# A fused attention and MLP kernel on one core: q/k weights loaded on ScalarE's queue, a run's product behind the gate, more moves on SyncE, and a reordered end

## The chip, the cores and the metric

The kernel runs on one core of a Trainium2 chip. The core has a matrix engine (TensorE, PE in the profile), VectorE (DVE), ScalarE (ACT), GpSimd (POOL) and SyncE (SP), each with its own instruction queue, and 16 DMA engines that move data between the chip's memory and SBUF, the on-chip memory. Matmul results go to PSUM, which has eight banks. A queue works in order: an instruction that waits holds up all behind it on the same engine. SP and ACT can issue DMAs, and so can POOL. The metric is the time of one execution in microseconds (us); "before" has a median of 200.42 us over three runs (200.35 to 201.31).

## The reference: what is computed

With `x` of 2048 positions and 512 columns in bf16, layer-normalised to `xn`:

```python
qkv = xn @ wqkv                                  # 32 heads of 16
logits[w] = q[s] . k[s - 2*w] * 16**-0.5         # w = 0..7, positions below 0 masked
s = (softmax(logits) . v) @ wo                   # sliding, dilated attention

h  = gelu(layernorm(xn) @ w1)                    # four column groups shifted by -1, +1, -2, +2
x1 = xn + shifted(h) @ w2
b  = x1 + gelu(layernorm(x1) @ w3) @ w4          # inner width 1376

out = x + s * silu(b)
```

The sliding window steps by two positions, so even and odd positions are two separate sequences; the kernel calls them p = 0 and p = 1, each with 1024 rows.

## The kernel before

**First part, to about 104 us.** The rows come in as `xn` tiles of 128 rows (`load_x`, L115). A chunk c is 512 rows of one sequence, and chunk 0 is loaded tile by tile, the others two tiles at a time. On SP the order is: two tiles of chunk 0, the first half of the q/k weights `wqk_sb` (L129), a tile, the second half, the last tile, then chunks 1 and 2, `w1` and chunk 3. Each half of the weights has two of the four blocks of 128 contraction rows, 512 KB; a tile of x has 128 KB. DVE and ACT normalise the tiles, TensorE transposes them (`first_columns`, L272, and `columns`, L259), and `qk` (L282) makes q and k. Its very first group of matmuls takes the blocks of the first weight half for two outputs, and then those of the second half. After it come w1, the shifted w2 and w3 for all four chunks, with gelu on ACT.

**The loop, n = 0 to 15.** The attention is done in 17 units (`order`, L56). Unit 0 has the first 64 rows of both sequences, every other unit 120 rows of one. Iteration n issues, in this order on the engines: `scores(n)` on TensorE (L605); `weighted(n-1)` (L638), which multiplies the weights `prob` with the values (L652) and takes the result out of PSUM bank o into `orw`: on DVE a small copy `mix` (L667) and an add (L668), and a wide copy, the "eviction" (`evict`), that is on ACT in the loop (L670); the exponentials on ACT (L616); `values(n+1)` on TensorE into bank b (L584); the gate of an earlier tile on DVE (L563); `within(n)`, the band mask, on DVE (L625); `w4_part(n)` on TensorE (L531) with its add on DVE (L539); and from n = 6 on `final`, the product with `wo` for one tile (L801, also in bank b), whose result DVE multiplies with the gate (L812), and POOL adds x (L817). All instructions of an engine keep the order of the source.

**Runs.** `orw` holds sums and row sums side by side. For a run (two units in a row; units 0 and 13 to 16 are runs of their own), the sums have to get into `oT`, with heads on the partitions: eight DMAs, one for each group of four heads (`moves`, L687; on SP and POOL). The row sums go out to `dn` (`sums_gather`), are inverted on DVE (L760) and written to memory, and are read back broadcast over the partitions (`sums_read`, L768, on SP). Then DVE multiplies `oT` by them: `sums_apply`, L776. With the run's last unit b, this is done in iteration b + 3, behind `within` and ahead of the add of `w4_part`. Head group 7 is moved one iteration after the others, ahead of `sums_read` on SP.

**The end, from n = 15 on.** The last runs have no time for those DMAs. R is 11, so R-3, R-2 and R-1 are the runs of units 14, 15 and 16, and R-4 that of unit 13. For R-3 to R-1 TensorE turns the row sums (`sums_turn`, L706), DVE inverts them (`sums_inverse`, L714), ACT spreads them (L719), TensorE turns them back (`sums_back`, L744) and DVE multiplies (`sums_mult`, L753). For R-2 and R-1, TensorE also does the move (`rows`, L731), with a copy on ACT (L736). `gate2` to `gate7` are the last six tiles; tile 7 is done in two halves of 256 columns, each added on DVE and stored from SP or ACT. For tile 6 the add of x is done by TensorE and ACT (`pe_add`, L831). In this part the eviction of unit 15 is on DVE (L671), and `load_xo` and `store` are DMAs on SP.

Of the kernel before, what the change touches and what calls it, by code (L numbers as in the profile page):

```python
# [15 lines left out]
def kernel(  # L16
# [19 lines left out]
    W = 8  # L36
# [87 lines left out]
    wqk_sb = midt([P, ND, 2 * D], "wqk_sb")  # L124
    x_tiles = load_x(0, 1)
    next(x_tiles)
    next(x_tiles)
    for dt in range(0, ND, 2):
        sp.dma_start(out=wqk_sb[:, dt : dt + 2, :], in_=wqkv_v[:, dt : dt + 2, 0 : 2 * D])  # L129
        next(x_tiles)  # L130
    list(load_x(1, 2))
# [12 lines left out]
    eps = const.tile([P, 1], F32, name="eps")  # L144
    dve.memset(eps[:], EPS)

    wm = psa("warm_ps")
# [489 lines left out]

    def weighted(n, eng=None):  # L638

# [19 lines left out]
        if p is None:  # L659
# [4 lines left out]
            t.tensor, t.offset + off, [list(t.ap[0]), [step, 2], list(t.ap[-2]), [1, width]]  # L664
        )
        mix = small.tile([P, 2 * ND, W], F32, name="mix", tag="mix")
        dve.tensor_copy(out=mix, in_=ov_[:, 1, :, 0:W])  # L667
        dve.tensor_tensor(out=ow[:, :, c + m : c + KB], in0=ov_[:, 0, :, m:KB], in1=mix, op=ALU.add)  # L668
        if eng is None:
            return lambda: act.activation(wide(ow, c, KB, m), wide(ov_, 0, CH + W, m), AF.Copy)  # L670
        return lambda: eng.tensor_copy(out=wide(ow, c, KB, m), in_=wide(ov_, 0, CH + W, m))  # L671

# [97 lines left out]

    def sums_apply(i):
        _, a, b, _, rw, parts = run_of(runs[i][0])
        rr = rden.pop(i).rearrange("p (s q) -> p s q", s=ND)
        for p, q0, c, nq in parts:
            o = oT[p][:, :, q0 : q0 + nq]
            dve.tensor_tensor(out=o, in0=o, in1=rr[:, :, c : c + nq], op=ALU.mult)  # L776

# [13 lines left out]
    def final(p, i, tags="b"):  # L791
# [15 lines left out]
        def mult(k, cs, pt):  # L807
# [8 lines left out]
            def add(eng):  # L816
                eng.tensor_tensor(out=x_o[:, cs], in0=sg, in1=x_o[:, cs], op=ALU.add)  # L817
                if len(pts) > 1:
                    (sp, act)[k % 2].dma_start(out=ov[p, i * P : (i + 1) * P, cs], in_=x_o[:, cs])

            return add

        def gate(eng):
            for k, (cs, pt) in enumerate(pts):
                gate.add = mult(k, cs, pt)
                if eng is not None:
                    gate.add(eng)

        return gate

    def pe_add(p, i, sg, tag):  # L831

        x_o = xo[p, i & ~1][:, i % 2, :]
        pt = pst(tag, "add_ps")[:, 0, :]
        pe.matmul(pt, lhsT=ident[:], rhs=x_o, start=True, stop=False)

        def rest():
# [5 lines left out]
    def store(q, p, i, n=2):  # L843
        q.dma_start(
                out=ov[p, i * P : (i + n) * P, :].rearrange("(i q) d -> q i d", q=P),
                in_=xo[p, i & ~1][:, i % 2 : i % 2 + n, :],
            )

# [6 lines left out]
    for n in range(NN - 1):  # L855
# [20 lines left out]
        for i in back:  # L876
            if 0 < i < R - NC - 1:
                moves(i, [sp], None, [7])
            sums_read(i)
        for i in done:  # L880
            if i == 0:
                moves(i, [sp, pool], 0)
            elif i < R - NC - 1:
                moves(i, [pool, sp, pool, pool, sp, pool, sp], None, range(7))
            elif i == R - NC - 1:
                moves(i, [pool], None, range(4))
            else:
                moves(i, [pool, pool, sp, pool])
        if n == NN - 2:
# [3 lines left out]
        late = [i for i, (a, b) in enumerate(runs) if n == max(b + 3, 5)]  # L893
        if n < NN - 2:
            for i in late:
                sums_apply(i)
        w4_part(n, 0, NF if n < NN - 2 else CUT)
# [8 lines left out]
        if gate:  # L906
            gate(pool)
        if n == NN - 3:
            moves(R - NC - 1, [pool], None, range(4, 8))
# [5 lines left out]
    scores(NN - 1)  # L915
    weighted(NN - 2, dve)()
    load_xo(1, 6)
    store(sp, 1, 0)
    exps(NN - 1)
    act.preload_act_table_set("silu_and_others")  # L920
    w4_part(NN - 2, CUT, NF)
    gate_silu(NN - 2)
    within(NN - 1)
    gate2 = final(1, 2, "b")
    layout("high", f=1, g=1, h=1, i=1)
    sums_turn(R - 2, "g")
    sums_inverse(R - 2, rows(R - 2, "h"))
    gate2(pool)
    sums_back(R - 3, "f")
    evict = weighted(NN - 1)  # L930
    sums_apply(R - 4)
    sums_mult(R - 3)
    evict()
    gate_silu(NN - 3)
    gate3 = final(1, 3, "i")
    gate3(pool)
    store(sp, 1, 2)
    gate4 = final(1, 4, "w")
# [57 lines left out]
```

## Time and profile before

| | us |
|---|---|
| median of three runs | 200.42 (200.35 to 201.31) |
| the profiled execution | 201.85 |
| its span, first to last instruction | 200.1 |
| TensorE busy | 188.8 (94%) |
| DVE busy | 127.0 (63%) |
| ACT busy | 125.3 (63%) |
| POOL busy | 63.5 (32%) |

The granted TensorE clock was 0.996 of full. All times in the text are from the start of the span. A line such as "140.75 0.66 DVE L776 TENSOR_TENSOR oT<-oT,orw ... [1.50 <-DMA orw<-rden_d]" says: at 140.75 us, for 0.66 us, on DVE, from line 776, tile `oT` made of `oT` and `orw`; ahead of it the engine was idle for 1.50 us, and that ended with the landing of a DMA into `orw`. SPq and ACTq are an engine's queue issuing a DMA, which is not counted as busy. In a list of waits the three numbers are the total, the number of waits and the longest. The chain of waits is followed back from the last instruction, at each step to what released it.

### The profile page before, as it was taken

To read this page: it belongs to the slowest core of one execution; us is meant where nothing else is said; L and a number is where in the kernel's file an instruction comes from. 1 tells how busy PE (TensorE), PEld (TensorE's weight loads), DVE (VectorE), ACT (ScalarE), POOL (GpSimd) and SP (SyncE) were. 2 spreads that over 40 slices of the span, in tenths; PEclk is the share of its full clock that TensorE was granted. 3 is DMA by queue.
4 is the path that set the end of the run, shared out by engine and by line. 5 is a ranking of instruction groups with operands and counts; after the bars stand their busy time and mean duration, and the time that the engine had idled before them with its cause. 6 is when DMAs were issued, how large, how long until landed. Compare 5 with 4: busy or idle time off the path is not lost.

```text
span 200.1 us, 6140 instructions
## 1 busy us (share of the span) xinstructions
PE 188.8 (94%) x2563; PEld 98.5 (49%) x2589; DVE 127.0 (63%) x250; ACT 125.3 (63%) x137; POOL 63.5 (32%) x121
## 2 busy tenths in 40 slices
PE   7699999999999999999999999999899999999790
PEld 2488754444444444444445555455455555555450
DVE  4688876228449968200005777786878787878982
ACT  3279849645820534666568788877757776677921
POOL 4055724700200120100000704124426262669460
PEclk9999999999999999999999999999999999999998
DMA  5973181479262266340510113122232251523443
GB/s 165 336 233 98 45 275 55 132 186 349 64 156 56 105 144 169 109 105 0 178 58 0 21 15 79 59 54 59 52 111 50 56 156 49 157 44 97 121 157 108
DMA packets 32748, 22.32 MB, mean 112 GB/s; under 512 B 17072, under 2 KB 31696, under 8 KB 32720
## 3 DMA queue, kind: packets, MB, share of 16 engines
q1 hardware_dynamic: 30960, 20.71, 35.9%
q0 software_dynamic: 1472, 1.02, 2.6%
q8 instruction: 20, 0.33, 0.7%
q10 hardware_dynamic: 288, 0.20, 0.3%
q14 instruction: 8, 0.07, 0.1%
HBM read 12.41 MB, written 4.83 MB: 86 GB/s over the span
## 4 chain that ended last, share of the span: by engine, by line
PE 76%; DMA 8%; DVE 5%; ACT 4%; SPq 3%; issue 2%; DVEq 0%; ACTq 0%
PE w_ps L396 17%; PE qk_ps L299 14%; PE w_ps L531 12%; PE w_ps L356 7%; PE w_ps L332 7%; PE v_ps L584 7%; DMA oT<-orw 4%; PE wo_ps L801 4%; PE o_ps L652 3%; DMA wqk_sb<-in_A_wqkv_dram 3%; ACT orw L670 2%; PE s_ps L605 2%; SPq L682 1%; PE w_ps L412 1%; PE tr_ps L266 1%
## 5 line engine op out<-in xcount | busy, mean ns | idle before, releaser
L616 ACT ACTIVATE prob<-s_ps 128x2048 bf16<-128x2048 f32 (+1 forms) x18 | 32.0, 1781 | 18.8 <-PE s_ps L605 18.8
L531 PE MATMUL w_ps<-w_sb,h3T 128*128 128x512 bf16 (+1 forms) x174 | 40.4, 379 | 0.3 <-issue 0.3
L696 POOL DMA_DIRECT2D oT<-orw x46 | 23.6, 519 | 49.8 <-DVE orw L660 30.3
L400 ACT ACTIVATE h3T<-w_ps 128x1024 bf16<-128x1024 f32 x20 | 20.5, 1024 | 24.9 <-PE w_ps L396 24.9
L396 PE MATMUL w_ps<-x1nT,w_sb 128*128 128x512 bf16 x156 | 34.8, 379 | 0.2
L299 PE MATMUL qk_ps<-xnT,wqk_sb 128*128 128x256 bf16 (+1 forms) x191 | 29.3, 308 | 1.3 <-DMA wqk_sb<-in_A_wqkv_dram 0.8
L531 PEld LDWEIGHTS <-h3T 128*128 128x128 bf16 (+1 forms) x176 | 17.0, 98 | 20.4
L396 PEld LDWEIGHTS <-w_sb 128*128 128x128 bf16 x160 | 15.5, 98 | 19.1 <-issue 0.4
L299 PEld LDWEIGHTS <-wqk_sb 128*128 128x128 bf16 x192 | 18.4, 98 | 11.1 <-DMA wqk_sb<-in_A_wqkv_dram 1.1
L625 DVE TENSOR_TENSOR prob<-prob,band 128x2048 bf16<-128x2048 bf16 (+1 forms) x18 | 21.4, 1191 | 2.3 <-ACT prob L616 2.3
L306 ACT ACTIVATE qT<-qk_ps,sel 128x1024 bf16<-128x1024 f32 x16 | 16.7, 1113 | 6.3 <-PE qk_ps L299 6.3
L584 PE MATMUL v_ps<-wv_sb,xnT 128*128 128x512 bf16 x49 | 15.8, 381 | 1.4 <-DVE sg L812 0.6
L801 PE MATMUL wo_ps<-wo_sb,oT 128*128 128x512 bf16 (+1 forms) x67 | 16.2, 366 | 0.9 <-DVE oT L776 0.7
L361 DVE TENSOR_TENSOR xn<-w_ps,xn 128x1024 bf16<-128x1024 f32 x8 | 9.7, 1211 | 11.5 <-PE w_ps L356 11.5
L817 POOL TENSOR_TENSOR xo<-sg,xo 128x512 bf16<-128x512 bf16 x9 | 10.4, 1153 | 20.7 <-DVE sg L812 20.2
L587 DVE CAST v_aug<-v_ps 128x512 bf16<-128x512 f32 x1 | 0.7, 692 | 22.5 <-ACT h3T L400 22.5
L356 PE MATMUL w_ps<-w_sb,hT 128*128 128x512 bf16 x63 | 14.3, 379 | 0.1
L332 PE MATMUL w_ps<-xn2T,w_sb 128*128 128x512 bf16 x62 | 14.2, 379 | 0.1
L539 DVE TENSOR_TENSOR xn<-w_ps,xn 128x512 bf16<-128x512 f32 x15 | 10.3, 690 | 5.9 <-PE w_ps L531 5.8
L670 ACT ACTIVATE orw<-o_ps 128x896 bf16<-128x896 f32 x15 | 13.7, 913 | 0.3 <-issue 0.3
L652 PE MATMUL o_ps<-prob,v_aug 64*32 64x64 bf16 x1088 | 12.5, 196 | 0.4 <-DVE prob L625 0.3
L215 POOL TENSOR_SCALAR l3r<-l3m 128x4 f32<-128x4 f32 x4 | 0.9, 229 | 35.9 <-DVE l3m L211 35.9
(99 smaller groups left out, 242.9 us busy)
## 6 DMA issues: line engine op xcount, KB each, us to landing
x1n_dram<-xn SPq DMA_DIRECT2D x4, 512.0 KB
xo<-in_A_x_dram SPq DMA_DIRECT2D x8, 256.0 KB
out_dram<-xo SPq DMA_DIRECT2D x7, 256.0 KB
xn<-in_A_x_dram SPq DMA_DIRECT2D x6, 256.0 KB
orw<-rden_d SPq DMA_DIRECT2D x6, 240.0 KB
w_sb<-in_B_w_dram SPq DMA_DIRECT2D x1, 1376.0 KB
w_sb<-in_B_w_dram SPq DMA_DIRECT2D x1, 1280.0 KB
wqk_sb<-in_A_wqkv_dram SPq DMA_DIRECT2D x2, 512.0 KB
```

The costliest lines, as they stand in the source:

```text
L299: pe.matmul(pt[:, b, :], lhsT=wqk_sb[:, dt, nt * P : (nt + 1) * P], rhs=xnT[p][:, dt, ms], start=(dt == 0), stop=(dt == ND - 1),)
L332: pe.matmul(pt[:, b, :], lhsT=w1_sb[:, dt, g * P : (g + 1) * P], rhs=xn2T[:, dt, :], start=(dt == 0), stop=(dt == ND - 1),)
L356: pe.matmul(pt[:, j, :], lhsT=w2_src(p, g, m0), rhs=w2_sb[:, g, :], start=(g == 0), stop=(g == ND - 1),)
L396: pe.matmul(pt[:, b, :], lhsT=w3_sb[:, dt, ft * P : (ft + 1) * P], rhs=x1nT[:, dt, :], start=(dt == 0), stop=(dt == ND - 1),)
L400: act.activation(h3_tile(c)[:, 2 * a : 2 * a + 2, :], pt, AF.Gelu_apprx_tanh)
L531: pe.matmul(pt, lhsT=h3[c][:fs, ft, jj * P : (jj + 1) * P], rhs=w4_sb[:fs, ft, :], start=(ft == 0), stop=(ft == NF - 1 and t < NN - 2),)
L584: pe.matmul(vp, lhsT=xnT[p][:, dt, k0 : k0 + P], rhs=wv_sb[:, dt, :], start=first, stop=last)
L616: act.activation(pr[:, rs_], t[:, rs_], AF.Exp, scale=SCALE)
L625: dve.tensor_tensor(out=w, in0=w, in1=b.unsqueeze(1).to_broadcast([P, m, KB]), op=ALU.min)
L652: pe.matmul(op[32 * cg : 32 * cg + 32, s, g * KB : (g + 1) * KB], lhsT=va[KB * s : KB * s + KB, dt * 8 + h, :], rhs=pr[KB * s : KB * s + K ...
L696: queues[hh % len(queues)].dma_start(out=oT[p][DH * hh : DH * (hh + 1), :, q0 : q0 + nq], in_=w[32 * cg : 32 * cg + DH, ND * jj : ND * jj ...
L801: pe.matmul(pt, lhsT=oT[p][:, dt, i * P : (i + 1) * P], rhs=wo_sb[:, dt, cs], start=(dt == 0), stop=(dt == ND - 1),)
```

## The change

Six things, in the order of the source.

1. All x tiles are issued on SP without the weights between them. The two DMAs of the q/k weights are issued on ACT, after the load of its table, and a memset of one column of each block by DVE comes ahead of them, which they have to wait for.
2. In the loop, up to n = 13, `sums_apply` of a run comes behind `final` and its gate.
3. Of a run's eight moves POOL issues 0, 2 and 4 and SP 1, 3 and 5, and then 6 and 7 one iteration later (before: POOL four, SP three, then one). For unit 14 in iteration 15, POOL and SP issue four each (before: six and two).
4. The eviction of unit 15 is on ACT behind the exponentials, not on DVE.
5. The end has a new order. Two things of it are new work for an engine: `sums_apply(R - 4)` is on POOL, and the first half of tile 7 is added by TensorE and ACT, as tile 6 is.
6. Both row copies come behind the spread sums on ACT (before: that of R-2 came ahead).

```diff
     wqk_sb = midt([P, ND, 2 * D], "wqk_sb")
-    x_tiles = load_x(0, 1)
-    next(x_tiles)
-    next(x_tiles)
-    for dt in range(0, ND, 2):
-        sp.dma_start(out=wqk_sb[:, dt : dt + 2, :], in_=wqkv_v[:, dt : dt + 2, 0 : 2 * D])
-        next(x_tiles)
+    list(load_x(0, 1))
     list(load_x(1, 2))
...
+    dve.memset(wqk_sb[:, :, 0:1], 0.0)
+    for dt in range(0, ND, 2):
+        act.dma_start(out=wqk_sb[:, dt : dt + 2, :], in_=wqkv_v[:, dt : dt + 2, 0 : 2 * D])
...
-    def weighted(n, eng=None):
+    def weighted(n, first=lambda: None):
...
+        first()
         mix = small.tile([P, 2 * ND, W], F32, name="mix", tag="mix")
...
-    def sums_apply(i):
+    def sums_apply(i, eng=dve):
...
-    def pe_add(p, i, sg, tag):
+    def pe_add(p, i, tag, cs):
...
-                moves(i, [sp], None, [7])
+                moves(i, [sp], None, [6, 7])
...
-                moves(i, [pool, sp, pool, pool, sp, pool, sp], None, range(7))
+                moves(i, [pool, sp], None, range(6))
...
             else:
-                moves(i, [pool, pool, sp, pool])
+                moves(i, [pool, sp])
...
         within(n, 2 if n == 0 else 1)
         late = [i for i, (a, b) in enumerate(runs) if n == max(b + 3, 5)]
-        if n < NN - 2:
-            for i in late:
-                sums_apply(i)
         w4_part(n, 0, NF if n < NN - 2 else CUT)
...
         if gate:
             gate(pool)
+        if n < NN - 2:
+            for i in late:
+                sums_apply(i)
...
     scores(NN - 1)
-    weighted(NN - 2, dve)()
+    evict = weighted(NN - 2)
     load_xo(1, 6)
     store(sp, 1, 0)
     exps(NN - 1)
+    evict()
     act.preload_act_table_set("silu_and_others")
...
     gate2 = final(1, 2, "b")
     layout("high", f=1, g=1, h=1, i=1)
+    sums_back(R - 3, "f")
+    gate3 = final(1, 3, "h")
+    sums_apply(R - 4, pool)
+    evict = weighted(NN - 1, first=lambda: gate2(pool))
+    evict()
     sums_turn(R - 2, "g")
-    sums_inverse(R - 2, rows(R - 2, "h"))
-    gate2(pool)
-    sums_back(R - 3, "f")
-    evict = weighted(NN - 1)
-    sums_apply(R - 4)
-    sums_mult(R - 3)
-    evict()
-    gate_silu(NN - 3)
-    gate3 = final(1, 3, "i")
+    sums_inverse(R - 2, rows(R - 2, "i"), True)
     gate3(pool)
     store(sp, 1, 2)
     gate4 = final(1, 4, "w")
+    sums_mult(R - 3)
+    sums_turn(R - 1, "g")
     sums_back(R - 2, "f")
+    sums_inverse(R - 1, rows(R - 1, "h"), True)
     sums_mult(R - 2)
-    sums_turn(R - 1, "g")
+    gate_silu(NN - 3)
     gate5 = final(1, 5, "b")
-    sums_inverse(R - 1, rows(R - 1, "i"), True)
     gate4(pool)
     gate5(pool)
     store(sp, 1, 4)
-    sums_back(R - 1, "h")
-    gate6 = final(1, 6, "w")
+    sums_back(R - 1, "i")
+    gate6 = final(1, 6, "g")
     sums_mult(R - 1)
+    halves = [slice(0, D // 2), slice(D // 2, D)]
+    add6 = pe_add(1, 6, "o", slice(0, D))
     gate6(None)
-    add6 = pe_add(1, 6, gate6.sg, "g")
-    gate7 = final(1, 7, "fb")
-    add6()
+    gate7 = final(1, 7, "fw")
+    add6(gate6.sg)
     store(act, 1, 6, 1)
-    gate7(dve)
+    add7 = pe_add(1, 7, "h", halves[0])
+    gate7.mult(0)
+    add7(gate7.sg)
+    store(sp, 1, 7, 1, halves[0])
+    gate7.mult(1)(dve)
+    store(act, 1, 7, 1, halves[1])
```

More of the change, by code (lines that the diff above doesn't have):

```diff
@@ L668, in weighted @@
         dve.tensor_tensor(out=ow[:, :, c + m : c + KB], in0=ov_[:, 0, :, m:KB], in1=mix, op=ALU.add)
-        if eng is None:
-            return lambda: act.activation(wide(ow, c, KB, m), wide(ov_, 0, CH + W, m), AF.Copy)
-        return lambda: eng.tensor_copy(out=wide(ow, c, KB, m), in_=wide(ov_, 0, CH + W, m))
+        return lambda: act.activation(wide(ow, c, KB, m), wide(ov_, 0, CH + W, m), AF.Copy)
     oT = {}
@@ L775, in sums_apply @@
             o = oT[p][:, :, q0 : q0 + nq]
-            dve.tensor_tensor(out=o, in0=o, in1=rr[:, :, c : c + nq], op=ALU.mult)
+            eng.tensor_tensor(out=o, in0=o, in1=rr[:, :, c : c + nq], op=ALU.mult)
     def slot():
@@ L817, in add @@
                 eng.tensor_tensor(out=x_o[:, cs], in0=sg, in1=x_o[:, cs], op=ALU.add)
-                if len(pts) > 1:
-                    (sp, act)[k % 2].dma_start(out=ov[p, i * P : (i + 1) * P, cs], in_=x_o[:, cs])
             return add
@@ L827, in gate, with rest @@
                     gate.add(eng)
+        gate.mult = lambda k: mult(k, *pts[k])
         return gate
-    def pe_add(p, i, sg, tag):
-        x_o = xo[p, i & ~1][:, i % 2, :]
-        pt = pst(tag, "add_ps")[:, 0, :]
+    def pe_add(p, i, tag, cs):
+        x_o = xo[p, i & ~1][:, i % 2, cs]
+        pt = pst(tag, "add_ps")[:, 0, cs]
         pe.matmul(pt, lhsT=ident[:], rhs=x_o, start=True, stop=False)
-        def rest():
+        def rest(sg):
             pe.matmul(pt, lhsT=ident[:], rhs=sg, start=False, stop=True)
@@ L841, in pe_add, with store @@
         return rest
-    def store(q, p, i, n=2):
+    def store(q, p, i, n=2, cs=slice(0, D)):
         q.dma_start(
-                out=ov[p, i * P : (i + n) * P, :].rearrange("(i q) d -> q i d", q=P),
-                in_=xo[p, i & ~1][:, i % 2 : i % 2 + n, :],
-            )
+            out=ov[p, i * P : (i + n) * P, cs].rearrange("(i q) d -> q i d", q=P),
+            in_=xo[p, i & ~1][:, i % 2 : i % 2 + n, cs],
+        )
     final_at = {n: divmod(n - 6, 8) for n in range(6, 16)}
```

## The prediction

> **What bounds the kernel now.** I read the page first, for the busy shares and the granted clock, then the chain of waits in order of time, TensorE's own waits, and the timeline of the three places where TensorE stands still.
>
> ```profile
> span 200.1 us, 6140 instructions
> ...
> PE 188.8 (94%) x2563; PEld 98.5 (49%) x2589; DVE 127.0 (63%) x250; ACT 125.3 (63%) x137; POOL 63.5 (32%) x121
> ```
>
> TensorE is busy for 188.8 of 200.1 us at a granted clock of 0.996. No matmul of the main body goes away, so all that can be won is in the 11.3 us in which it stands, or is handed out again there. The chain says where the kernel follows something other than TensorE:
>
> ```profile
> 2.70 5.42 DMA wqk_sb<-in_A_wqkv_dram
> ...
> 8.17 2.36 PE qk_ps L299 x20
> ...
> 184.78 1.00 DVE orw L671
> 185.77 1.73 DVE prob L625
> ...
> 194.30 1.09 DVE slots L810 x2
> ```
>
> The q/k weights hold the start, and VectorE (DVE) holds the end from 182.7 on. TensorE's waits put prices on the places:
>
> ```profile
> PE qk_ps L299 <- DMA wqk_sb<-in_A_wqkv_dram: 0.8, 1, 0.8
> PE wo_ps L801 <- DVE oT L776: 0.7, 1, 0.7
> PE v_ps L584 <- DVE sg L812: 0.6, 1, 0.6
> ```
>
> The third one is in the loop. In the timeline a run's product L776 stands on DVE until its row sums arrive, so L539 and the gate L812 are late, and the next `values` matmul finds bank b still in use:
>
> ```profile
> 140.75 0.66 DVE L776 TENSOR_TENSOR oT<-oT,orw 128x960 bf16<-128x960 bf16 x1 [1.50 <-DMA orw<-rden_d]
> ...
> 142.66 1.02 PE L584 MATMUL v_ps<-wv_sb,xnT 128*128 128x512 bf16 x3 [0.59 <-DVE sg L812]
> ```
>
> The end, from the timeline:
>
> ```profile
> 184.69 1.08 DVE L671 CAST orw<-o_ps 128x896 bf16<-128x896 f32 x1
> ...
> 185.24 1.17 POOL L817 TENSOR_TENSOR xo<-slots,xo 128x512 bf16<-128x512 bf16 x1
> ...
> 185.69 1.81 DVE L625 TENSOR_TENSOR prob<-prob,band 128x2048 bf16<-128x2048 bf16 x1
> ...
> 189.18 0.37 SPq L789 DMA_DIRECT2D xo<-in_A_x_dram  x1
> ...
> 196.80 0.34 ACTq L819 DMA_DIRECT2D out_dram<-xo  x1
> ```
>
> L625 takes 1.81 us here and 1.21 in every other iteration: it meets POOL's L817 for 0.7 us and loses 0.6. L563 (0.63 alone, 0.93 at 158.94 beside L817) and the half-size L776 at 188.98 (0.89, where 960 elements take 0.66) show the same. A DVE operation with two SBUF inputs stands while POOL runs a tensor operation; L812, which reads PSUM, keeps 0.68. POOL can lose too: L216 takes 1.87 at 22.40 beside DVE's L315, else 0.72.
>
> **The change, part by part.**
>
> *Start.* Two 0.43 us issues leave SP, so the x tiles behind them are issued up to 0.9 us earlier. That is worth nothing by itself: from 8.17 to 14 TensorE stands for less than 0.1 us, and SP is idle from 8.5 to 13.07. On ScalarE (ACT) the two issues lie ahead of the first root at 4.12, on DVE the memset (0.06, as L143) ahead of an idle stretch. What counts is when the second weight half lands, since TensorE waits from 7.35 to 8.17. Its issue was at 2.70. It now follows the memset (about 1.1) and may have to stand behind the table load that ends at 2.07, so the halves go out at 1.2 and 1.65 or at 2.1 and 2.55. Against this, the x tiles no longer queue behind the weights but move beside them. Before, 1408 KB had moved when that half was in (three tiles of 128, two halves of 512). Shared byte for byte from the second tile on it is 128 + 2048 = 2176 KB. Shared row for row it is 1664, for a row of weights has 1024 columns and a row of x 512. At the 365 GB/s of 4 to 8 us these are 2.2 and 0.7 us later, less the 0.5 to 1.0 by which the issues are earlier. The other end is the whole wait, 0.8 us gained, if whole transfers alternate. No row of this trace has two queues loading at once. Rows being what the engines move one by one, I take the middle: 0.7 less 0.7, **0.0**; ends -0.8 and +2.2.
>
> The Trainium skill (DMA: Bandwidth & Descriptors, "Queues, rings and completion order") says that each DMA engine goes round the queues packet by packet, a packet being some 9 to 17 descriptors. One tile (128 rows over 16 engines) or one half (256) is about that, so by this rule the old order would stay, and this term would be -0.8.
>
> *Loop.* The product of a run goes behind the gate. The 1.50 us stand then lies where bank b is already free: **-0.6**. What comes late instead is the next iteration's `mix` L667. Its DVE work has 0.57 idle before L539 and 0.24 before L812 (156.46 and 157.40), and `values` starts 0.10 after L812, so 0.9 us of delay costs nothing. The product now stands beside POOL's L817. If DVE is first (it needs no semaphore, and POOL started 0.08 after L812's end at 163.45), `mix` is 0.15 late: cost 0. If POOL is first, the product waits 1.15 and `mix` is 1.35 late: 0.45 each in four iterations (7, 9, 11, 13), +1.8. I take **0.0**, as DVE is the nearer one.
>
> The Trainium skill (SBUF — State Buffer, "SBUF: two separate sides") calls the pair of ports that DVE and GpSimd share an exclusive lock, held for an instruction by whichever starts first. The rows above agree; by it this term is 0 as well, and +1.8 if POOL's start comes first.
>
> Of a run's eight moves, SP issues five (four before) and POOL three. One more SP issue (0.65) lies ahead of the row-sum read L768, which waits for its own write anyway (4.9 us in all); if it is late by all of 0.65, the product that reads it is 1.8 us later than before (163.3 for 161.5 in iteration 11). Cost 0.
>
> *End*, in times of this trace. (1) POOL issues 8 moves instead of 10 (L696, 0.51 each) and is free at 184.2, so its L817 runs from 184.4 to 185.6 and no longer meets L625. That starts at 185.65, when L616's `prob` is done (183.75 + 1.86), and ends at 186.86 instead of 187.50: -0.64. Run 7's product, now on POOL (1.08, from 1.15 for 512 columns), must not come first. Its row sums are requested at 182.63; 240 KB of them took 4.3 and 5.3 us (157.21 to 161.51, 135.46 to 140.75), a single move 2.1, so 120 KB arrive between 184.7 and 187.9, with 186.3 in the middle. If they are early, L625 ends at 187.9. (2) The copy L671 (1.08) goes from DVE to ACT as L670 (0.91). L625 waits for `prob` whichever it is, so nothing is won there. ACT's table load and Silu come 0.9 later, and the next eviction starts at 188.4 instead of 188.88. (3) DVE's list behind `mix` and the add, which end at 188.3 (188.81 before): two reciprocals 0.7, three gates 1.95, three products L753 1.95, L810 0.68 + 0.42 + 0.42, one half add 0.29, together 6.4. Of the 7.96 before, L776 (0.89), one half add and the 0.40 stand ahead of it are gone, and one reciprocal has moved in. With 0.3 of waits for ACT's copies the list ends at 195.0, not 196.77. (4) ACT now has the last word: copy of tile 6 (0.60) to 195.05, its store's issue 0.38, a half copy 0.35, and the last store is issued at 195.85, where the last one was at 196.80: -0.95. (5) Two more moves on SP (0.65 each) push the last x load from 189.18 to 190.5. It arrives 2.4 (the first tile, 0.80 to 3.17) to 2.8 us later, near 193.2; TensorE's add would want it at 192.75: +0.25. End: **-0.7**, from -0.95 to +0.4.
>
> Four more half matmuls (0.22 each) lie in TensorE's idle end.
>
> Sum: 0.0 - 0.6 - 0.7 = -1.3. The profiled execution took 201.85 (span 200.1 and 1.75 around it), 0.7% over the median of 200.42. It becomes 200.55, and the median **199.1**.
>
> **The rivals.**
>
> *Weights sooner.* Whole transfers alternate and the 0.8 wait goes: 198.3. For it: the issues are up to a microsecond earlier, and the engines moved only 184 GB/s from 3 to 4 us. Against: the weights now share from their first row.
>
> *Weights late (slower).* Byte-for-byte sharing brings the second half 2.2 later: 199.1 + 2.2 = 201.3, and 202 if the table load holds the issue as well. It decides once that half lands more than 1.3 us later, after 9.5. For it: the engines are full from 4 us on, so what x gains the weights lose. Against: weight rows are twice as long.
>
> *POOL first in the loop.* +1.8 gives 200.9. For it: POOL held the port in every meeting of the loop. Against: there DVE arrived in the middle of L817.
>
> *No gain at the end.* The row sums of run 7 arrive before 185.6, POOL takes the port ahead of L625, and the end is at +0.3 instead of -0.7: 200.1. For it: the lower bound of 184.7. Against: the 4.3 us and more of the larger reads.
>
> **How the numbers follow.** 0.5% of 200.42 is 1.0 us, about what a measurement of this kernel can tell from no change. Forecast 0.40 (198.6 to 199.6, three quarters of it below 199.4), weights sooner 0.20, no gain at the end 0.15, POOL first 0.13, weights late 0.12. Faster: 0.30 + 0.20 = 0.50. Slower: 0.07 of the weights and 0.03 of POOL, 0.10. The rest, 0.40, is within 0.5%. From weights sooner to POOL first the range is 198.2 to 200.9; left out are the late weights and what lies beyond the ends.
>
> **What would show it.** Start: the wait of L299 for `wqk_sb`, 0.82 now; gone means weights sooner, over 2 means late. Loop: no L584 wait for L812, L776 with no stand ahead of L812; L776 at over 1.5 us would be POOL first. End: L625 at 185 or so back at 1.21, L776 on POOL behind it, last store issued 0.7 to 0.95 earlier, counted from L625's start. The prediction is wrong if TensorE waits more than 2 us for the weights, or if the end moves to ACT's row copies or to the last x load and gives back more than 0.7.

## The result, and the profile after

The changed kernel takes 203.45 us in the median (201.80 to 205.02, six runs), the kernel before 200.69 (200.35 to 201.31, six runs beside them). The ratio is 1.0103, with a 95% interval of 1.0056 to 1.0150. Ratios, here and below, leave out runs over 1.5% above the fastest of the same kernel (of after these are 204.90 and 205.02, at granted clocks of 0.983 and 0.972) and medians do not, so differences are taken from the ratios, where 1% is 2.0 us. The prediction was 199.1, from 198.2 to 200.9: it was wrong, by 4.35 us and by the sign.

The two profiled executions don't show the size of the loss. The one of after took 201.80, the least of its runs, and the one of before 201.85, more than all of its own. They show where it lies. The head of the page of after:

```profile
span 200.1 us, 6164 instructions
...
PE 190.5 (95%) x2591; PEld 98.6 (49%) x2591; DVE 125.0 (62%) x248; ACT 126.6 (63%) x139; POOL 61.8 (31%) x114
```

The span is the same to the tenth. TensorE's own waits in after (total, number, longest):

```profile
PE add_ps L832 <- DMA xo<-in_A_x_dram: 2.2, 1, 2.2
PE tr_ps L276 <- DVE xn L225: 1.4, 1, 1.4
PE warm_ps L148 <- DVE wqk_sb L142: 1.1, 1, 1.1
PE qk_ps L298 <- DVE xnT L278: 0.4, 1, 0.4
```

Of the waits that the prediction started from, those for the weights, for `oT` and for the gate (0.8, 0.7 and 0.6 us) are gone. Two others are there instead: 2.2 us for the last x load, and 1.4 for the transposes at the start, which stood for 0.5 before. The start, from the timeline of after:

```profile
1.13 0.97 ACTq L144 DMA_DIRECT2D wqk_sb<-in_A_wqkv_dram  x2
...
5.50 0.69 DVE L209 BATCH_NORM_STATS2 l1s<-xn 128x6 f32<-128x512 bf16 x1 [1.56 <-DMA xn<-in_A_x_dram]
...
6.97 0.92 PE L276 MATMUL tr_ps<-ident,xn 128*128 128x128 bf16 x8 [1.40 <-DVE xn L225]
...
8.29 2.78 PE L298 MATMUL qk_ps<-xnT,wqk_sb 128*128 128x256 bf16 x24 [0.40 <-DVE xnT L278]
```

The first 24 products now run without a break, so nothing waits for the weights any more. What is late is x tile 1: DVE reads it at 5.50, where it read it at 4.00 before, and the transposes wait for it. The 24 products end at 11.07 instead of 10.53. The end, from the same timeline:

```profile
183.20 0.64 SPq L766 DMA_DIRECT2D orw<-rden_d  x1
...
183.89 2.62 SPq L694 DMA_DIRECT2D oT<-orw  x4
...
184.96 1.48 DVE L624 TENSOR_TENSOR prob<-prob,band 128x2048 bf16<-128x2048 bf16 x1 [0.45 <-ACT prob L615]
...
186.56 0.58 SPq L787 DMA_DIRECT2D xo<-in_A_x_dram  x1
...
187.25 0.41 SPq L841 DMA_DIRECT2D out_dram<-xo  x1
...
191.25 0.37 SPq L787 DMA_DIRECT2D xo<-in_A_x_dram  x1
...
194.37 0.38 PE L832 MATMUL add_ps<-xo,ident 128*128 128x512 bf16 x1 [2.21 <-DMA xo<-in_A_x_dram]
```

This is SP's list: the read of the row sums, four moves (two before), a load of x, a store, and the last load of x, which goes into the buffer that the store empties and so has to wait until the store has landed. The chain of waits of after runs over just these steps:

```profile
187.25 3.98 DMA out_dram<-xo
...
191.25 3.08 DMA xo<-in_A_x_dram
...
194.37 0.38 PE add_ps L832
```

Before, DVE's list held this stretch.

### The profile page after: what moved, and what is told of

Same layout as the page of the kernel before. It is cut to its first block, busy times and chain, and to the rows that moved or that the text cites. A ratio compares the mean times of both kernels' runs of the same rounds, so it can differ in the third digit from the quotient of the medians.

```text
span 200.1 us, 6164 instructions
## 1 busy us (share of the span) xinstructions
PE 190.5 (95%) x2591; PEld 98.6 (49%) x2591; DVE 125.0 (62%) x248; ACT 126.6 (63%) x139; POOL 61.8 (31%) x114
## 4 chain that ended last, share of the span: by engine, by line
PE 87%; DMA 6%; DVE 2%; ACT 2%; issue 0%; SPq 0%; ACTq 0%; POOL 0%; POOLq 0%
PE w_ps L530 19%; PE w_ps L395 17%; PE qk_ps L298 14%; PE v_ps L583 8%; PE w_ps L331 7%; PE w_ps L355 7%; PE wo_ps L799 5%; PE o_ps L651 5%; PE s_ps L604 3%; DMA xn<-in_A_x_dram 2%; DMA out_dram<-xo 2%; DMA xo<-in_A_x_dram 2%; PE w_ps L411 1%; PE tr_ps L265 1%; ACT prob L615 1%; DVE prob L624 1%
## 5 line engine op out<-in xcount | busy, mean ns | idle before, releaser
L694 POOL DMA_DIRECT2D oT<-orw x38 | 19.4, 519 | 50.0 <-DVE orw L659 30.3
L815 POOL TENSOR_TENSOR xo<-sg,xo 128x512 bf16<-128x512 bf16 x9 | 11.8, 1306 | 21.1 <-DVE sg L810 21.1
L583 PE MATMUL v_ps<-wv_sb,xnT 128*128 128x512 bf16 x64 | 16.6, 381 | 0.0
L669 ACT ACTIVATE orw<-o_ps 128x896 bf16<-128x896 f32 x16 | 14.6, 912 | 0.2 <-PE dt_ps L704 0.2
L209 DVE BATCH_NORM_STATS2 l1s<-xn 128x6 f32<-128x512 bf16 x16 | 10.7, 671 | 2.8 <-DMA xn<-in_A_x_dram 2.8
L335 ACT ACTIVATE hT<-w_ps 128x1024 bf16<-128x1024 f32 x8 | 8.2, 1028 | 6.2 <-PE w_ps L331 6.2
```

What stands on the lines that cost most here:

```text
L583: pe.matmul(vp, lhsT=xnT[p][:, dt, k0 : k0 + P], rhs=wv_sb[:, dt, :], start=first, stop=last)
L694: queues[hh % len(queues)].dma_start(out=oT[p][DH * hh : DH * (hh + 1), :, q0 : q0 + nq], in_=w[32 * cg : 32 * cg + DH, ND * jj : ND * jj ...
```

## The experiments

In all kernels the computation is whole. The medians are of all runs, the ratios are to the kernel before, run beside each of them. Three marks in the profiled execution cut it into stages: (a) the start of the first `exps` of 2048 columns (109.46 in after); (b) from there to the start of the last band multiplication (`within`, 184.96 in after); (c) from there to the end of the last store's issue (197.71 in after, two issues of SP that begin at 193.56 and take 4.15). That execution is not always a typical one: those of after, e2, e3 and e13 are the fastest of their runs, those of e7 and e12 the slowest.

| kernel | median us | ratio, 95% interval | a | b | c |
|---|---|---|---|---|---|
| before | 200.69 | | 109.06 | 76.63 | 11.45 |
| after | 203.45 | 1.0103 (1.0056 to 1.0150) | 109.46 | 75.50 | 12.75 |
| e1: after, old start | 202.31 | 1.0064 (1.0034 to 1.0093) | 109.38 | 75.74 | 13.29 |
| e3: after, last load free of the store | 200.35 | 0.9986 (0.9957 to 1.0014) | 109.16 | 75.55 | 10.50 |
| e5: both | 199.22 | 0.9930 (0.9907 to 0.9953) | 108.79 | 75.78 | 11.18 |
| e15: e5 again | 199.29 | 0.9926 (0.9902 to 0.9951) | 108.86 | 75.89 | 11.12 |
| e10: e1, unit 14's moves as before | 199.49 | 0.9953 (0.9926 to 0.9979) | 108.64 | 75.71 | 11.01 |
| e12: e5, unit 14's moves as before | 199.82 | 0.9941 (0.9914 to 0.9967) | 108.81 | 76.19 | 14.69 |
| e14: before, unit 14's moves new | 203.30 | 1.0118 (1.0087 to 1.0149) | 108.73 | 75.78 | 14.44 |
| e2: before, new start | 202.23 | 1.0056 (1.0028 to 1.0085) | 109.17 | 75.70 | 11.42 |
| e6: e2, 13 warm-ups | 201.05 | 1.0011 (0.9991 to 1.0032) | 109.12 | 75.97 | 11.43 |
| e7: before, 7 warm-ups | 201.21 | 1.0034 (1.0003 to 1.0065) | 110.80 | 76.03 | 11.43 |
| e8: before, x tile 1 on ACT too | 201.16 | 1.0010 (0.9980 to 1.0040) | 108.31 | 76.22 | 11.43 |
| e9: e5 with e8's start | 199.88 | 0.9949 (0.9919 to 0.9979) | 108.64 | 76.28 | 11.01 |
| e13: after, unit 14's moves as before | 202.73 | 1.0096 (1.0058 to 1.0135) | 110.32 | 75.71 | 10.99 |
| e18: e13 again | 201.86 | 1.0054 (1.0033 to 1.0075) | 110.55 | 75.67 | 10.98 |
| e17: e13, 13 warm-ups | 200.63 | 0.9998 (0.9978 to 1.0018) | 109.33 | 76.14 | 11.15 |
| e4: before, product behind the gate | 200.86 | 1.0006 (0.9977 to 1.0036) | 108.46 | 75.95 | 11.42 |
| e11: e5, product ahead of the gate | 200.01 | 0.9968 (0.9939 to 0.9997) | 108.54 | 76.83 | 10.49 |
| e16: e11 again | 199.63 | 0.9948 (0.9929 to 0.9968) | 108.49 | 76.08 | 10.78 |

**The end.** My theory after the first profile was that the last x load costs the 2.2 us of TensorE's wait, and the late tile 1 the rest. e1 gives the start its old order:

```diff
-    list(load_x(0, 1))
+    x_tiles = load_x(0, 1)
+    next(x_tiles)
+    next(x_tiles)
+    for dt in range(0, ND, 2):
+        sp.dma_start(out=wqk_sb[:, dt : dt + 2, :], in_=wqkv_v[:, dt : dt + 2, 0 : 2 * D])
+        next(x_tiles)
...
-    dve.memset(wqk_sb[:, :, 0:1], 0.0)
-    for dt in range(0, ND, 2):
-        act.dma_start(out=wqk_sb[:, dt : dt + 2, :], in_=wqkv_v[:, dt : dt + 2, 0 : 2 * D])
```

> The changed kernel with the start of the kernel before: weights on SP, behind two x tiles. In the trace of the changed kernel x tile 1 is read at 5.50 us where it was at 4.00, TensorE's first transposes come at 6.97 where they came at 5.43, and its median is 2.8 above the kernel before, of which that trace alone shows nothing (its execution is the fastest of its runs). Theory start: the late tile costs 0.4 us in every execution, and in some TensorE's clock comes up later as well; then this one is at 200.7 (200.69, less 1.1 for the loop, plus 1.0 for the late x load at the end) with a clock of 0.996 or more in all runs. Theory end: the 2.2 us in which TensorE waits for the last x tiles are what costs, and what varies; then it is at 203.0, 0.4 below the changed kernel.

e3 puts the x rows of tiles 6 and 7 into spare columns of another buffer, so that their load needs no landed store:

```diff
-        xo[p, i] = xop.tile([P, 2, D], BF16, name="xo", tag="xo")
+        if (p, i) == (1, 6):
+            xo[p, i] = banks["slots"][0][:, 14:16, :]
+        else:
+            xo[p, i] = xop.tile([P, 2, D], BF16, name="xo", tag="xo")
```

> The changed kernel, but the x rows of the last two tiles go to spare columns of the slots tile, so that their load does not wait for the store of an earlier buffer (3.98 us on SP). Both theories: the wait of TensorE for the last x load, 2.2 us, goes, and the last store comes 1.7 to 2.2 earlier. Theory start: 201.5 at the median, clocks spread from 0.97 to 1.0 as before. Theory end: 200 or less, clocks all at 0.996 or more.

e5 has both edits, and e15 is e5 once more.

> Both: the start of the kernel before, and the last x load without its wait. Theory start: 198.8 (200.69, less 1.1 for the loop and 0.8 for the end), and faster than the kernel before by 0.9%. Theory end: as the one with the load alone, less 0.4.

> The version with both repairs once more, beside the next kernel on one chip: 199.2.

e1 came out between its two forecasts. With the load free, the loss at the end is gone: by the ratios e3 lies 2.3 us under after, and e5 2.7 under e1. The two edits together have the lowest medians, 199.22 and 199.29 us, 0.7% under the kernel before; 0.7 us of waiting for that load is left in them. In e3's timeline the load leaves right behind the store, four microseconds sooner than in after, and the add doesn't wait:

```profile
187.07 0.47 SPq L790 DMA_DIRECT2D slots<-in_A_x_dram  x1
...
191.88 0.38 PE L835 MATMUL add_ps<-slots,ident 128*128 128x512 bf16 x1
```

That the load is late is settled by this; not yet what makes it late. e10 takes e1 and gives unit 14's moves back to POOL:

```diff
-                moves(i, [pool, sp])
+                moves(i, [pool, pool, sp, pool])
```

> The changed kernel with the start as before, and the moves of unit 14 shared as before (three by GpSimd, one by SyncE in each four, instead of two and two). Beside it stands the changed kernel with the old start alone: 202.31 us, its last add waits 2.4 us for the last x load. Theory that the two more moves on SyncE's queue push that load: each took 0.6 to 0.7 us of SyncE's queue, the load leaves 1.3 us sooner, the add's wait falls to about 1.1 us, and the time to about 201.0. Rival, that the load is late for the wait on the last store of the tile before it and for the sums' trip through memory, whatever the number of moves: the wait stays at 2 us or more and the time at 202.0 to 202.6. If both lie in it, between the two.

It gained 1.1%, 2.2 us, where I had expected 1.3, and is faster than before although SP's list still has the store ahead of the load. e10's timeline:

```profile
183.23 1.34 SPq L696 DMA_DIRECT2D oT<-orw  x2
...
184.35 1.85 DVE L626 TENSOR_TENSOR prob<-prob,band 128x2048 bf16<-128x2048 bf16 x1 [0.52 <-ACT prob L617]
...
184.62 0.58 SPq L789 DMA_DIRECT2D xo<-in_A_x_dram  x1
...
185.30 0.41 SPq L843 DMA_DIRECT2D out_dram<-xo  x1
...
188.73 0.37 SPq L789 DMA_DIRECT2D xo<-in_A_x_dram  x1
...
191.89 0.38 PE L834 MATMUL add_ps<-xo,ident 128*128 128x512 bf16 x1
```

Counted from the band multiplication, the load leaves at 4.38, in e1 at 6.10 (191.22 less 185.12). 1.3 of these 1.7 us are the two issues, the rest is the store, which landed in 3.43 us here and in 3.83 there. e14 is the same line in reverse, alone in the kernel before:

```diff
-                moves(i, [pool, pool, sp, pool])
+                moves(i, [pool, sp])
```

> The kernel before, with that one line of the change alone: unit 14's moves shared two and two by GpSimd and SyncE. Before, the last x load left at 189.18 us, landed some 2.8 us later, and the add that wants it began at 194.10. Theory that the line costs only where the rest of the change has drawn the last add ahead: here the load lands near 193.3, still ahead of the add, and GpSimd's sum no longer meets the band multiplication: 200.0 to 200.7, no slower. Rival, that two more moves on SyncE's queue cost by themselves (the store and load behind them): 201.5 or more.

I had expected it to be harmless there, as the add before began 2 us after the load had landed. It cost 1.2%, by itself as much as the whole change. Its timeline:

```profile
182.26 3.17 SPq L696 DMA_DIRECT2D oT<-orw  x4
...
184.51 1.22 DVE L625 TENSOR_TENSOR prob<-prob,band 128x2048 bf16<-128x2048 bf16 x1
...
185.48 0.59 SPq L789 DMA_DIRECT2D xo<-in_A_x_dram  x1
...
186.17 0.41 SPq L844 DMA_DIRECT2D out_dram<-xo  x1
...
191.37 0.37 SPq L789 DMA_DIRECT2D xo<-in_A_x_dram  x1
...
194.81 0.43 PE L835 MATMUL add_ps<-xo,ident 128*128 128x512 bf16 x1 [2.33 <-DMA xo<-in_A_x_dram]
...
196.74 0.63 PE L838 MATMUL add_ps<-slots,ident 128*128 128x512 bf16 x1
```

The band multiplication doesn't meet POOL and takes 1.22, as the prediction had it. But the store needs 5.20 us to land (3.36 in before), the add stands for 2.33, and then TensorE's clock has fallen: it is granted at 0.50 from 195.0 on, and the last add takes 0.63 us, where it takes 0.38 with the full clock. So a stand of 2.3 us costs 3.0 (c is 14.44 for 11.45), with the 0.6 won at the multiplication already in it. e12 asks what the shared moves are worth when nothing waits for the load (e5 with e10's edit).

> The version with both repairs (199.22 us) with the moves of unit 14 shared as before, three by GpSimd and one by SyncE. The x load can't be late here, so this shows what the sharing of the moves is worth by itself. Theory of the prediction (GpSimd's sum for tile 5 then meets VectorE's band multiplication, 0.64 us): 199.8. Rival, that the gain of the end comes from the order of VectorE's and ScalarE's work alone: 199.2. Third: the moves' two places less on SyncE's queue are worth more than the meeting costs: below 199.0.

The ratios differ by 0.1%, which their intervals don't tell from nothing, so the 0.64 us that the prediction put on the meeting isn't shown in the times; the 0.6 in the medians (199.82 for 199.22) comes from three long runs among e12's twelve. Its profiled execution, the slowest of them (203.81), shows what the meeting did there, and its c of 14.69 is not the usual end of this kernel:

```profile
184.59 1.17 POOL L820 TENSOR_TENSOR xo<-slots,xo 128x512 bf16<-128x512 bf16 x1
...
185.00 2.89 DVE L626 TENSOR_TENSOR prob<-prob,band 128x2048 bf16<-128x2048 bf16 x1 [0.89 <-ACT prob L617]
...
187.94 0.68 PE L653 MATMUL o_ps<-prob,v_aug 64*32 64x64 bf16 x64 [1.42 <-DVE prob L626]
```

Here the multiplication stood behind POOL's add and then behind run 7's product too; TensorE stood for 1.42, and from 189.0 to 195.8 its granted clock was 0.50.

**The start.** e2 is the new start alone in the kernel before (e1's edit in reverse).

> The kernel before with the new start alone. Theory start: 203, clocks from 0.97 to 1.0, TensorE idle for 1.4 us ahead of the first transposes. Theory end: 201.1 (0.4 for the late tile), clocks as in the kernel before. If the weights' sharing with x is all there is to it, x tile 1 is late here too and the second weight half lands before 8.2.

It costs 0.56%, about 1.1 us, but its a is only 0.1 later than before's, in its fastest execution. The runs showed a second thing: 7 of e2's 12 had a mean granted clock of 0.986 to 0.988, while 29 of the 31 runs of before beside it had 0.995 or more. So e6 adds three warm-up matmuls to e2, and e7 takes three from the kernel before:

```diff
-    for i in range(10):
+    for i in range(13):
```

> The kernel before with the new start and 13 warm-up matmuls instead of 10, so that TensorE works until about 6.6 us and idles 0.1 to 0.3 instead of 1.1 to 1.4 ahead of the first transposes. Theory clock: the new start costs 0.4 for the late x tile, and the rest because in half of the executions the granted clock is 0.987 instead of 0.995 and more; here nearly all clocks are at 0.995 or more, and the median is at 201.2. Rival: the clock has nothing to do with that idle time; 202.2 and clocks as without the three matmuls.

> The kernel before with 7 warm-up matmuls instead of 10: TensorE idles from 4.1 to 5.4, and nothing that it waits for is later. Theory clock: half of the executions at 0.987, median 201.7. Rival: 200.7, clocks at 0.995 and more as in the kernel before.

With 13 the clock is at 0.994 or more in all 12 runs and the loss is gone but for 0.1%. With 7, before loses 0.3%, in the direction that the theory of the clock gives, though by half of what I had put on it; two of its twelve runs have a mean clock under 0.99, where I had expected six. But the mean doesn't show everything. e7's profiled execution took 202.96 us with a mean of 0.999, and its a, 110.80, is the latest of all. The 20 products that took 2.36 us in before's took 4.45 here:

```profile
7.87 4.45 PE L299 MATMUL qk_ps<-xnT,wqk_sb 128*128 128x256 bf16 x20 [0.23 <-DMA wqk_sb<-in_A_wqkv_dram]
```

The trace's record of the granted clock begins at 13.0 us in this execution (at 4.1 in before's), and the mean counts the time ahead of the record as full, although the matmuls ran at half their pace there. So a clock that comes late at the start is not in the mean at all. e8 avoids the late tile, with x tile 1 ahead of the weights on ACT:

```diff
-    x_tiles = load_x(0, 1)
-    next(x_tiles)
-    next(x_tiles)
+    def x_one(q, t):
+        q.dma_start(out=xn[0][:, t, :], in_=xv[0, t * P : (t + 1) * P, :])
+
+    x_one(sp, 0)
+    x_one(act, 1)
     for dt in range(0, ND, 2):
-        sp.dma_start(out=wqk_sb[:, dt : dt + 2, :], in_=wqkv_v[:, dt : dt + 2, 0 : 2 * D])
-        next(x_tiles)
+        act.dma_start(out=wqk_sb[:, dt : dt + 2, :], in_=wqkv_v[:, dt : dt + 2, 0 : 2 * D])
+    x_one(sp, 2)
+    x_one(sp, 3)
```

> The kernel before with the weights on ACT's queue, behind x tile 1 that is on the same queue, without the memset; SP issues tiles 0, 2, 3 and the rest. Theory sharing: with the weights behind it tile 1 has the engines to itself and tile 0, is read at 4.0 or sooner, TensorE starts its transposes at 5.4, and the wait for the second weight half is 0.8 or less: 200.2 to 200.7, clocks at 0.995 and more. Rival: loads from a second queue are slow as such; 202.

e9 is e5 with this start.

> The changed kernel with the last x load free of the store (as in the version with both repairs, 199.22 us), and with a third order at the start: x tile 1 and both halves of the q/k weights on ScalarE's queue, tile 1 first, no memset. The same start in the kernel before gave 201.16 against 200.65, 0.1 to 0.5% more, at a full clock. Theory that the start costs only through a late tile and a late clock: tile 1 is no longer behind weight rows, its share of this is gone, 199.0 to 199.5. Rival, that weights on ScalarE's queue cost by themselves: 199.9 or more, about what the kernel before showed on top of 199.22.

Neither can be told from the old start (e8 from before, e9 from e5), though a is 0.1 to 0.5 earlier than 108.78, the mean of the ten executions with the old start and ten warm-ups. e13 and e18, one kernel measured twice, have e10's edit in the changed kernel, beside its new start; e17 has 13 warm-ups too.

> The changed kernel with one line undone: the moves of unit 14 are shared as before (three by GpSimd, one by SyncE, in place of two and two); its new start stays. The same line undone beside the old start took 202.31 to 199.49 us. Theory that SyncE's two more moves cost 2.2 us and the start 1.1 (each by its own comparison): from 203.45 to about 200.6, level with the kernel before. Rival, that the x load is late for the start as well (a later loop shifts SyncE's list at the end): above 201.5.

> The changed kernel with unit 14's moves shared as before (202.73 us so far, but 199.49 with the old start as well) and 13 warm-up matmuls in place of 10. In the kernel before, three more warm-ups took the new start's cost from 1.6 us to 0.4. Theory that the new start costs by a late clock there too: about 200. Rival, that something else holds the new start's executions up, the last x load or what lies between: above 201.5.

> The changed kernel with unit 14's moves shared as before, once more and beside the one with 13 warm-ups: 202.7 if the first measurement holds; 200.6 if it was high. Its profile is of another execution: by the theory of the clock the mean clock is near 0.988 and no add waits; by the rival the add waits 2 us for the last x load although SyncE has two moves fewer.

The new start costs 2.0 to 2.9 us here (ratios of 1.0054 and 1.0096 for e10's 0.9953), more than in e2, and three warm-ups take 1.1 of it away (0.9998 for 1.0054, on the same chip). In their profiles c is back at 11.0, no add waits, and all of the loss is in a. The start of e18, a wait of the transposes and the timeline:

```profile
PE tr_ps L276 <- DVE xn L225: 2.1, 1, 2.1
```

```profile
5.56 0.69 DVE L209 BATCH_NORM_STATS2 l1s<-xn 128x6 f32<-128x512 bf16 x1 [1.70 <-DMA xn<-in_A_x_dram]
...
7.02 1.11 PE L276 MATMUL tr_ps<-ident,xn 128*128 128x128 bf16 x8 [2.07 <-DVE xn L225]
...
8.43 4.03 PE L298 MATMUL qk_ps<-xnT,wqk_sb 128*128 128x256 bf16 x24 [0.30 <-DVE xnT L278]
```

The same of e17:

```profile
5.31 0.69 DVE L209 BATCH_NORM_STATS2 l1s<-xn 128x6 f32<-128x512 bf16 x1 [1.36 <-DMA xn<-in_A_x_dram]
...
6.77 0.92 PE L276 MATMUL tr_ps<-ident,xn 128*128 128x128 bf16 x8
...
8.10 2.78 PE L298 MATMUL qk_ps<-xnT,wqk_sb 128*128 128x256 bf16 x24 [0.40 <-DVE xnT L278]
```

The tile is as late in both. But ten warm-ups end at 4.94 in e18 and leave TensorE standing for 2.07 us, and the 24 products then take 4.03 us instead of 2.78: the granted clock of e18 is full from 4.2 us, 0.50 from 7.6 to 11.0, and then full again (e13's is 0.50 from 7.5 to 10.9). In e17 the warm-ups last until the transposes, and the clock is full from 6.4 on. What stays open: four of e13's seven runs had a mean clock of 0.997 or more and still took 202.4 to 204.0. A clock that came as late as in e7's profiled execution would not show in that mean, but none of the four is a profiled one.

**The loop.** e4 is the product behind the gate, alone in the kernel before; e11 and e16 (one kernel twice) undo it in e5:

```diff
-        if n < NN - 2:
-            for i in late:
-                sums_apply(i)
         w4_part(n, 0, NF if n < NN - 2 else CUT)
...
         if gate:
             gate(pool)
+        if n < NN - 2:
+            for i in late:
+                sums_apply(i)
```

> The kernel before with the runs' products behind the gate, nothing else. The term of the prediction: 0.6 us faster, 200.1, and no wait of the values matmul for the gate. Rival: the 1.50 us stand of L776 belonged to that one profiled execution (201.85, while 29 of 31 others were below it); in most executions the row sums are there in time, and this kernel is at 200.7 as before. If POOL takes the port first, 202.

> The version with both repairs (old start, x load free of the store; 199.22 us) with the product of a run ahead of the gate again, as it was before the change. Theory that the product's place is worth nothing in a usual execution (alone in the kernel before it gave 200.86 against 200.65): 199.0 to 199.5. Rival, the prediction's term of 0.6 us, which shows only where the end has no wait of its own: 199.8.

> The version with both repairs and the product of a run ahead of the gate, as before the change, once more, beside the version that has it behind the gate. Theory that the product's place is worth nothing in the median: within 0.3 us of its neighbour. Rival, the prediction's term, 0.6 us: 0.5 to 0.8 us above its neighbour, as in the first measurement (200.01 against 199.22, on another day's chip).

The ratios give +0.1 us for e4, and -0.4 (e15 against e16, one chip) to -0.8 (e5 against e11) in the repaired version; e4's can't be told from before, nor can the two of either pair be told apart. Stage b is finer: over the eight profiled executions with the product ahead of the gate it is 75.70 to 76.83, mean 76.16, over the twelve with it behind 75.50 to 76.28, mean 75.84. That is -0.3 us, with ranges that overlap. The wait for the gate shows in three of the eight (0.6 in before) and in none of the twelve. e11 has the longest, 1.3 us in two waits:

```profile
PE v_ps L585 <- DVE sg L815: 1.3, 2, 0.9
```

## Why the prediction was wrong

**Start, 0.0: wrong; about +1 us.** The step that failed is "What counts is when the second weight half lands". By the semaphore events of the trace that half had landed in full at 7.45 us in after, 0.7 sooner than before (8.13); over the profiled executions it is 7.45 to 7.80 with the new start and 7.42 to 8.47 with the old one. The 0.8 wait is gone, and the products begin at 8.29 anyway. But the sharing makes x tile 1 late, which until then had ridden ahead of the weights: it had landed in full at 5.48 instead of 3.45 and was read 1.5 us later, of which the 0.8 wait paid back a part. I had looked at what the weights lose to x and not at what x loses to the weights.

The middle that I took, "Shared row for row", was wrong too. Tile 0 has 128 rows, and 28 to 52 weight rows move before tile 1 gets going; row for row, at least 330 rows of x would then be in with the 256th weight row, the last of the first half. In the seven profiled executions with the new start it is 247 to 256, which is tiles 0 and 1. So a whole half moved for a whole tile, which was the other end of my term. The packet records don't name the DMA engine, so the order on one engine is not shown.

This is nearer to the rule of the Trainium skill (DMA: Bandwidth & Descriptors, "Queues, rings and completion order") that I weighed there, engines taking turns by packets of 9 to 17 descriptors. That "the old order would stay" doesn't follow from it: tile 1 stands behind tile 0 on SP's queue, so its 8 rows on an engine come after the half's 16. At 0.084 us a row, the median in this trace, that is an estimate of 1.3 us from the page's rule, and tile 1 was read 1.5 us later.

The second half of the loss was not in the sum at all: TensorE stands between its warm-ups and the transposes, and in some executions its clock falls back for 3.4 us. The means of stage a show it: 108.78 with the old start, 109.73 in the five with the new one (+0.95), 109.22 in the two with 13 warm-ups (+0.45). Of the five, the three whose clock stays full have +0.4 to +0.7, the two whose clock falls (e13, e18) +1.5 to +1.8. So the late tile is about half of it.

On the clock, the Trainium skill (TensorE: Matmul & The Clock Gate, "Part 1: The HAM clock gate (the "warmup" mystery)") says that the clock doubles after a busy window of about 3.4 us, and that these windows run freely and don't begin anew with the kernel. These runs agree in kind: the same start shows 24 products in 2.78 us (after) and in 4.03 (e18, only the shared moves differing). The page puts the cost under 1% of a kernel; here it is 0.5 to 0.6% (e2 against e6, e18 against e17), half of the change's loss.

**Loop, -0.6: the mechanism right, the size at most half.** The term took the one stand of 0.6 us in the profiled execution as every execution's. It occurs in three of eight; the mean gain in stage b is 0.3, and e4's time shows none. The bounds -0.6 and +1.8 held, and DVE first, the choice between them, was right: in after's four meetings the product kept its 0.65 us and POOL's add took 1.50 instead of 1.15.

**End, -0.7: -0.95 right, +0.25 wrong.** Without a wait for the load, c falls from 11.45 to 10.50 (e3) and 10.49 (e11), which is the -0.95 of points (1) to (4). Of this, e10 and its like without the shared moves have 0.3 to 0.5 (c of 10.98 to 11.15), so the meeting of L625 and L817 was worth the other half. In after itself they still met, as the multiplication came sooner than I had it and POOL's add ran until 185.35: the multiplication took 1.48. The product of run 7 came on POOL at 186.21, where the row sums had been put at 186.3, as the multiplication was ending (186.44), so "No gain at the end" did not come about. Point (5) is the term that was mis-sized: the last x load, +0.25. It was to leave at 190.5, arrive near 193.2 and be wanted at 192.75. In after it left at 191.25, arrived at 194.3 and was wanted at 192.16. To the 0.45 by which it was late in my own times (193.2 against 192.75, of which my sum took 0.25), 0.75 came from SP's list, which I had moved by two issues and nothing else: the row sums' trip through memory (3.7 us from write to read, 2.6 before) kept SP where it was although the loop was earlier, and the store took 4.0 to land instead of 3.4. Another 0.3 came from the load's own landing (3.1 where I took 2.8 as the upper end), and 0.6 because the rest of the end was faster than I had it. Together 2.2 us in this execution, which is the fastest of after's six, and by the ratios 2.2 (e1 against e10) to 2.7 (e1 against e5), with the clock that falls after the stand. I wrote that the prediction is wrong if the end moves "to the last x load and gives back more than 0.7"; it did, but I gave the case no chance of its own. It should have had one: a wait on a landing, behind a list that gets longer, is fragile.

**The sum.** By stages: a +0.95, b -0.3, c +1.3 (after) to +1.8 (e1), where -0.7 was forecast. That is +2.0 to +2.5; measured were +2.1 (the ratio) and +2.8 (the medians). What isn't explained is that the two losses do not add up in the runs: from e10, the shared moves add 1.1% (e1), the new start 1.0 to 1.4% (e18, e13), and both together 1.5%, where 2.1 to 2.5 would be expected. The interval of after alone is 0.5% to each side, and no run tells whether more lies in it.

**The rivals.** "Weights late" was near, in that the sharing at the start cost time, but named the wrong transfer: nothing waited for the weights. Of "Weights sooner" the mechanism came, a half for a tile and the wait gone, but not the gain, since the products now waited for tile 1. "POOL first" and "No gain at the end" did not occur.

## What to carry to other kernels

A DMA that waits for the landing of another is priced with its whole chain (the issues ahead of it on its queue, the landing of what it waits for, its own landing), and its slack is read as the smallest that the trace shows, because landings of the same store took 3.3 to 5.2 us here; a spare buffer (e5) or a shorter list ahead of it (e10) took the loss away. When loads are moved to another queue, ask of every load, and not only of those moved, when it now lands. And a new stand of TensorE, here of 1.4 to 2.4 us, is not over when the data arrive, as the clock may fall: look at how long the next matmuls take, let dummy matmuls last until the first real one, and don't take a mean clock near 1 for a proof that it came early.

## What the hardware showed that I had not expected

*The store's landing.* From the store's issue to the load that waits for it, the ten executions with two moves of unit 14 on SP and the load behind the store took 3.26 to 3.43 us, and the three with four moves 3.83, 4.00 and 5.20 (e1, after, e14). The packet records show one difference beside the issues: a load of instructions, one packet of 16 KB that takes 0.9 to 1.8 us. In the first ten it begins when at most 23 of the 512 packets of store and load have still to begin. In after and e1 it begins ahead of the first of them, and in e14 it comes with 19 still to begin; 16 packets end only after it there, up to 1.8 us behind the others. That the moved issues push the transfers into this load is argued from these executions; no run moved the load alone.

*ACT's first DMA.* ACT's two issues of the weights went out at 1.13 us, while its table load ran from 0.79 to 2.07. The prediction had held it possible that they must wait for 2.07.

*DVE and POOL, one at a time.* In e5 DVE started first and POOL stood:

```profile
184.57 1.23 DVE L626 TENSOR_TENSOR prob<-prob,band 128x2048 bf16<-128x2048 bf16 x1 [0.88 <-ACT prob L617]
...
184.88 1.87 POOL L776 TENSOR_TENSOR oT<-oT,orw 128x480 bf16<-128x480 bf16 x1 [0.35 <-DMA orw<-rden_d]
```

POOL's product takes 1.09 alone (e1, e3) and 1.87 here, 0.92 of it beside the multiplication, which keeps its 1.23. In e12 the order was the other way round, and the multiplication took 2.89.
